# Attention scores computed once in a two-layer transformer kernel

## The chip, the cores and the metric

The kernel runs on one core of one Trainium2 chip. The metric is the device time of one launch in microseconds. Before the change it is 2117.11 us, the median of two runs (2116.69 and 2117.53).

## The reference

The input x has 2048 tokens of 640 features. Two layers follow, with the same weights, and each layer has two residual blocks:

```python
x = x + _A_ref(_layernorm(x, axis=-1), A_wqkv, A_wo)   # attention
x = x + _B_ref(_layernorm(x, axis=-1), B_w1, B_b1, B_w2, B_b2)   # token mixer
```

Attention has 32 heads of 20 features. For each head it computes scores = q @ k^T / sqrt(20) over 2048 x 2048 pairs, their softmax, the product with v, and at the end a projection with `wo`. The mixer normalizes again, multiplies over the token axis with `w1` (2048 x 1536), adds a bias, applies a gelu, and multiplies back with `w2`.

## The kernel before

**Layout.** Heads are padded from 20 to 32 rows, so that four heads of a group fill 128 partitions; there are 8 groups. K (`KT`) and Q (`QTq`) are kept transposed, features on partitions. A score matmul works on 64 rows, which hold two heads. Masked copies of Q (`qev`, `qod`, made by `prep_block`) zero one of the two, so that one 64-row matmul gives the scores of a single head. Heads 0 and 1 use rows 0 to 63, heads 2 and 3 rows 64 to 127, and the order 0, 2, 1, 3 makes neighbours use different halves of the array, where they run side by side.

**Units, chunks and tiles.** A unit is one block of 512 queries, one group and one block of 128 keys: 4 x 8 x 16 = 512 units in a layer. Each unit gives four chunks, one for each head, of 128 keys x 512 queries. Three chunks in a row make a tile `S` of three PSUM banks, so that a layer has 683 tiles, four tiles for three units. There are two `S` buffers, six banks; the accumulator `acc` and the tile `misc` have one bank each.

**The loop of attention.** In the step for tile t, `attention` emits, in this order: the score matmuls of tile t+1 (`emit_S`, L317); the exponential of tile t on ScalarE (`emit_exp`, L345), which writes `P`; the product with V (`emit_PV`, L551) for every unit whose last tile is at least one step old, four matmuls that use 32 columns of the array each and run side by side; and then some fill matmuls (`emit_fills`). TensorE's order is fixed: every matmul is chained to the one before it. The scores of tile t+1 must wait until the exponential of tile t-1 has left their buffer, and an exponential waits for the last score matmul of its tile.

**Fills.** Work of TensorE that is not part of the loop above is queued and fed in between: projections of K and Q for later groups and blocks (L223), the output projection (L453, L486) and three quarters of the mixer's first multiplication (L426). A step without a P.V group takes up to 3 cost units of it, and one with a P.V group up to 1.5; a unit is a matmul of 512 columns. When a group of fill matmuls ends, VectorE copies it from `misc` and one step is left without fills. Where the queue is empty, or its first item not due, there are none either: in the profile the longest such stretches run from 456 to 515 us and from 678 to 746 us, and at 1505 and 1727 us in the second layer.

**The second pass.** Before a tile's scores are emitted, `planned_fill` says whether the current step will have fills. If not, `emit_S` runs with `reps` of 1: it issues the tile's three score matmuls twice, the second time over the same PSUM banks with the same result.

```python
has_fill = planned_fill()
reps = 0 if has_fill else CFG["R_DEFAULT"]
if t + 1 < NTILES:
    emit_S(t + 1, reps)
```

**Start.** GpSimd sets up the identity matrix for the transposes, two small constants, two bias transfers (L118, L119) and the rstd of each LayerNorm (L165) in one queue.

Of the kernel before, what the change touches and what calls it, by code (L numbers as in the profile page):

```python
# [11 lines left out]
BF16 = mybir.dt.bfloat16  # L12
# [12 lines left out]
VW = 24  # L25

CFG = dict(
    R_DEFAULT=1,
    FILL_NOPV=3.0,
    FILL_PV=1.5,  # L30
    PV_LAGT=1,
# [8 lines left out]
def kernel(  # L40
# [12 lines left out]
    nc = tc.nc  # L53
# [11 lines left out]
    def pe(inst):  # L65
        tc.chain_iter_dep("pe_order", inst.ins)
        return inst
# [12 lines left out]
    consts = ctx.enter_context(tc.tile_pool(name="consts", bufs=1))  # L80
# [16 lines left out]
    warm = consts.tile([128, 1], F32, name="warm")  # L97
    nc.gpsimd.tensor_tensor(out=warm[:], in0=mhalf[:], in1=mhalf[:], op=ALU.mult)
    nc.gpsimd.tensor_tensor(out=warm[:], in0=warm[:], in1=mhalf[:], op=ALU.pow)
    x1lp = ctx.enter_context(tc.tile_pool(name="x1lp", bufs=1))  # L100
    x1last = x1lp.tile([128, 4, D], F32, name="x1last")
    hhp = ctx.enter_context(tc.tile_pool(name="hhp", bufs=1))
# [137 lines left out]
    def attention(st, x_in_ap, x_mid, uacc_l):  # L240
        layer = st.layer
        KT, hT = st.KT, st.hT
        with ExitStack() as p1:
# [19 lines left out]
            S_tiles, P_tiles, acc_tiles, qm_tiles, attnT_tiles = {}, {}, {}, {}, {}  # L263
# [21 lines left out]
            def on_unit_start(n):  # L285
                qb_n, g_n, kt_n = units[n]
                fill_state["unit"] = n
                if qb_n == 0 and kt_n == 0:
                    if g_n + KQA < NG:
                        enqueue_kq_for_group(g_n + KQA)  # L290
                    if g_n == max(0, NG - KQA) and NQB > 1:
                        enqueue_qproj(1)
                if qb_n >= 1 and g_n == 0 and kt_n == 2 and qb_n + 1 < NQB:
                    enqueue_qproj(qb_n + 1)
                if not proj_enqueue_done[0]:
                    last_k_block = max(0, NG - 1 - KQA)
                    if NQB == 1:
                        done = (qb_n == 0 and g_n >= last_k_block)
                    elif NQB == 2:
                        done = (qb_n == 0 and g_n >= max(0, NG - KQA)) or qb_n >= 1  # L300
                    else:
                        done = (qb_n == NQB - 2 and (g_n > 0 or kt_n >= 2)) or qb_n > NQB - 2
                    proj_enqueue_done[0] = done
                check_hT_dead()
                if kt_n == 0:
                    ensure_ready(qb_n, g_n)
                    prep_block(qb_n, g_n)
                if kt_n == NKT // 2 and n + NKT < NU:
                    nqb, ng, _ = units[n + NKT - kt_n]
                    if ("Q", nqb, ng) not in pending_keys():  # L310
                        prep_block(nqb, ng)

            def s_matmul(St, slot, n, j):
                qb, g, kt = units[n]
                jj = j // 2
                q = qm_tiles[(qb, g)][j % 2]
                pe(nc.tensor.matmul(St[:, slot, :], lhsT=KT[64 * jj:64 * jj + 64, g, kt * 128:(kt + 1) * 128],  # L317
                                    rhs=q[64 * jj:64 * jj + 64, :], start=True, stop=True,
                                    tile_position=(64 * jj, 0)))

            def emit_S(t, reps):
                cs = chunks[3 * t:3 * t + 3]
                for (n, j) in cs:
                    if j == HORDER[0]:
                        on_unit_start(n)
                St = sps.tile([128, 3, 512], F32, name="S")
                S_tiles[t] = St
                for _rep in range(reps + 1):
                    i = 0
                    while i < len(cs):  # L330
                        n, j = cs[i]
                        if i + 1 < len(cs) and cs[i + 1][0] == n and (j, cs[i + 1][1]) in ((0, 2), (1, 3)):
                            s_matmul(St, i, n, j)
                            s_matmul(St, i + 1, n, cs[i + 1][1])
                            i += 2
                        else:
                            s_matmul(St, i, n, j)
                            i += 1

            def emit_exp(t):  # L340
                St = S_tiles.pop(t)
                ncs = len(chunks[3 * t:3 * t + 3])
                P = ptp.tile([128, 3, 512], BF16, name="P")
                P_tiles[t] = P
                nc.scalar.activation(out=P[:, 0:ncs, :].rearrange("p a b -> p (a b)"),  # L345
                                     in_=St[:, 0:ncs, :].rearrange("p a b -> p (a b)"),
                                     func=ACT.Exp, scale=SCALE)
# [194 lines left out]
            def emit_PV(n):  # L542
                qb, g, kt = units[n]
                if kt == 0:
                    acc_tiles[(qb, g)] = accp.tile([128, 512], F32, name="acc")
                acc = acc_tiles[(qb, g)]
                for j in range(4):
                    ci = 4 * n + HORDER.index(j)
                    P = P_tiles[ci // 3]
                    hh = 4 * g + j  # L550
                    pe(nc.tensor.matmul(acc[32 * j:32 * j + 32, :],  # L551
                                        lhsT=Vaug[:, (kt * H + hh) * VW:(kt * H + hh) * VW + 32],
                                        rhs=P[:, ci % 3, :], start=(kt == 0), stop=(kt == NKT - 1),
                                        tile_position=(0, 32 * j)))
                for t_ in list(P_tiles.keys()):
                    if (3 * t_ + 2) // 4 <= n:
                        del P_tiles[t_]
                if kt == NKT - 1:
                    normalize(qb, g, acc_tiles.pop((qb, g)))
                    if qb == LASTQB and PARTIAL_LAST:  # L560
                        if g % 2 == 1:
                            enqueue_outproj_partial(qb, g)
                    elif g == NG - 1:
                        enqueue_outproj(qb)

            def emit_fills(budget, pool_alloc):
                fs = fill_state
                if fs["cooldown"] > 0:
                    fs["cooldown"] -= 1
                    return 0.0  # L570
                spent = 0.0
                while spent < budget:
                    if fs["cur"] is None:
                        if not fill_queue:
                            break
                        if fill_queue[0].get("not_before", 0) > fs["unit"] and budget < 100:
                            break
                        fs["cur"] = fill_queue.popleft()
                        fs["idx"] = 0
                        fs["tile"] = pool_alloc()  # L580
                    grp = fs["cur"]
                    grp["mms"][fs["idx"]](fs["tile"])
                    spent += grp["cost"][fs["idx"]]
                    fs["idx"] += 1
                    if fs["idx"] == len(grp["mms"]):
                        grp["evac"](fs["tile"])
                        fs["cur"] = None
                        fs["cooldown"] = CFG["FILL_GAP"]
                        break
                return spent  # L590
# [4 lines left out]
            def planned_fill():  # L595
                if fill_state["cooldown"] != 0:
                    return False
                if fill_state["cur"] is not None:
                    return True
                return len(fill_queue) > 0 and fill_queue[0].get("not_before", 0) <= fill_state["unit"]  # L600

            LAGT = CFG["PV_LAGT"]
            pv_done = 0
            emit_S(0, 0)
            for t in range(NTILES):
                has_fill = planned_fill()
                reps = 0 if has_fill else CFG["R_DEFAULT"]
                if t + 1 < NTILES:
                    emit_S(t + 1, reps)
                emit_exp(t)  # L610
                n_pv = 0
                while pv_done < NU and (4 * pv_done + 3) // 3 <= t - LAGT:
                    emit_PV(pv_done)
                    pv_done += 1
                    n_pv += 1
                emit_fills(CFG["FILL_PV"] if n_pv else CFG["FILL_NOPV"], misc_alloc)
            in_attention[0] = False
            while pv_done < NU:
                emit_PV(pv_done)
# [148 lines left out]
    with ExitStack() as a_stack:  # L768
        st0 = open_a_scope(0, a_stack)
        with ExitStack() as p0:  # L770
# [29 lines left out]
            setup_wo()  # L800
            setup_biases()
        attention(st0, A_x[0], xd[0], uacc[0])
    with ExitStack() as a_stack:
        st1 = open_a_scope(1, a_stack)
# [59 lines left out]
```

## Time and profile before

| | |
|---|---|
| median of two runs | 2117.11 us |
| span of the profiled execution, first to last instruction | 2114.4 us |
| its distance to the two timed runs | 2.3 and 3.1 us |
| TensorE busy | 1950.4 us (92%), 13278 matmuls |
| ScalarE busy | 1934.5 us (91%), 1508 instructions |
| VectorE busy | 623.7 us (29%) |
| GpSimd busy | 166.4 us (8%) |
| mean granted TensorE clock | 0.990 |
| chain that ended last: the exponential (L345) | 56% of the span |
| the same: score matmuls (L317) | 11% |

The profiled execution has no time of its own beside the span; the table sets the span against the timed runs. Attention takes 48 to 972 us in the first layer and 1097 to 2021 us in the second; the start, the mixers and the end fill the rest. In the rows of tenths each digit is a fortieth of the span, about 53 us. The clock row shows which share of TensorE's full clock was granted. In the lines of groups, the numbers after the bar are the busy time of the group, the mean length of one in ns, and the idle time before them with what ended most of it. Instructions of one engine overlap, so the busy time is less than count times length: 1366 exponentials of 1501 ns are busy for 1839.6 us. The length of a matmul includes its flight through the array, so that a matmul of 512 columns is listed with about 0.38 us while the next can start after 0.215 us.

### The profile page before, as it was taken

The page shows a single profiled execution, that of the slowest core. Times are in us where ns is not written, and L with a number is a line of the kernel's source. Part 1 is how long each engine was busy: PE and PEld are TensorE (multiplying, and loading weights), DVE is VectorE, ACT ScalarE, POOL GpSimd, SP SyncE. Part 2 cuts the span into 40 slices and gives each one's busy share as a digit, 9 for nine tenths or more (in the row PEclk, how much of TensorE's full clock was granted, in tenths as well). Part 3 has the DMA queues.
Part 4 walks back from the last instruction along what each step waited for, and adds up shares of the span by engine and source line. Part 5 has one row for each costly group of instructions (what it writes and reads, how often), then busy time and mean ns, then how long its engine had stood idle before and what let it go on. Part 6 is the DMA issues. An engine that isn't in the chain of part 4 may idle for free.

```text
span 2114.4 us, 32063 instructions
## 1 busy us (share of the span) xinstructions
PE 1950.4 (92%) x13278; PEld 655.8 (31%) x13278; DVE 623.7 (29%) x1391; ACT 1934.5 (91%) x1508; POOL 166.4 (8%) x250
## 2 busy tenths in 40 slices
PE   7999999999999999996999999999999999999969
PEld 4222222233223323222542222222332233232235
DVE  6122233212422042223642122432123221422252
ACT  5999999999999999995349999999999999999952
POOL 2000000110012001100000000001000110111000
PEclk9999999999999999998999999999999999999989
DMA  5000000110034012223620000101100430232145
GB/s 129 1 1 1 1 20 19 63 51 10 29 64 64 1 38 43 39 40 96 212 81 1 1 1 1 38 21 65 41 26 26 75 53 1 57 53 37 32 120 181
DMA packets 90739, 96.89 MB, mean 46 GB/s; under 512 B 9696, under 2 KB 68192, under 8 KB 90592
## 3 DMA queue, kind: packets, MB, share of 16 engines
q1 hardware_dynamic: 70464, 71.22, 10.9%
q0 software_dynamic: 20128, 23.62, 7.4%
q8 instruction: 104, 1.70, 0.3%
q14 instruction: 43, 0.35, 0.1%
HBM read 55.48 MB, written 39.32 MB: 45 GB/s over the span
## 4 chain that ended last, share of the span: by engine, by line
ACT 56%; PE 26%; issue 12%; DVE 3%; DMA 1%; POOL 0%; SPq 0%; POOLq 0%; ACTq 0%; DVEq 0%
ACT P L345 56%; PE S L317 11%; PE y L746 4%; PE acc L551 4%; PE misc L223 3%; PE pp L214 1%; PE misc L453 1%; DVE bnst L158 1%; DMA ua<-uacc_65 0%; DVE bnst L159 0%; DMA ua<-uacc_66 0%; POOL rstd L165 0%; PE S L486 0%; DVE utmp L685 0%; PE pp L223 0%
## 5 line engine op out<-in xcount | busy, mean ns | idle before, releaser
L345 ACT ACTIVATE P<-S 128x1536 bf16<-128x1536 f32 (+1 forms) x1366 | 1839.6, 1501 | 9.8 <-PE S L317 8.3
L317 PE MATMUL S<-qev,KT 64*128 64x512 bf16 x2962 | 836.2, 377 | 97.4 <-ACT P L345 91.6
L317 PE MATMUL S<-qod,KT 64*128 64x512 bf16 x3052 | 838.0, 379 | 7.9 <-ACT P L345 3.7
L317 PEld LDWEIGHTS <-KT 64*128 64x128 bf16 x6014 | 326.4, 93 | 657.0 <-issue 487.8
L551 PE MATMUL acc<-P,Vaug 128*32 128x512 bf16 x4096 | 409.9, 389 | 6.2 <-ACT P L345 1.9
L551 PEld LDWEIGHTS <-Vaug 128*32 128x32 bf16 x4096 | 106.5, 92 | 439.0 <-issue 439.0
L432 DVE COPY ustg<-misc 128x512 f32<-128x512 f32 (+1 forms) x144 | 70.0, 486 | 291.8 <-PE misc L426 291.7
L165 POOL TENSOR_TENSOR rstd<-veps,mhalf 128x1 f32<-128x1 f32 x96 | 54.0, 563 | 1194.1 <-DVE veps L163 1167.1
L426 PE MATMUL misc<-h2st,w1st 128*128 128x512 bf16 (+1 forms) x576 | 116.1, 303 | 1.8 <-DVE h2st L170 1.8
L746 PE MATMUL y<-uT,w2s 128*128 128x512 bf16 (+1 forms) x768 | 107.6, 299 | 3.4 <-ACT uT L689 1.4
L513 DVE CAST QTq<-misc 128x512 bf16<-128x512 f32 x62 | 42.8, 691 | 205.5 <-PE misc L223 205.5
L513 DVE CAST KT<-misc 128x512 bf16<-128x512 f32 x56 | 38.7, 691 | 212.0 <-PE misc L223 207.8
L223 PE MATMUL misc<-hh,wq_pad 128*128 128x512 bf16 x310 | 98.9, 385 | 0.0
L276 DVE TENSOR_SCALAR qev<-QTq,mask_ev 128x512 bf16<-128x512 bf16 x64 | 22.5, 352 | 228.7 <-PE S L317 228.2
L223 PE MATMUL misc<-hh,wk_pad 128*128 128x512 bf16 x280 | 87.2, 385 | 0.0
L453 PE MATMUL misc<-wo_pad,attnT 128*128 128x512 bf16 (+1 forms) x384 | 76.8, 303 | 0.0
L746 PEld LDWEIGHTS <-w2s 128*128 128x128 bf16 x768 | 59.6, 98 | 49.9 <-issue 5.1
L76 ACT CAST Vaug<-pp 128x500 bf16<-128x500 f32 (+1 forms) x32 | 14.3, 453 | 50.8 <-PE pp L214 50.8
L437 POOL DMA_DIRECT2D uacc_66<-ustg x48 | 41.3, 860 | 232.7 <-DVE ustg L432 215.3
L437 POOL DMA_DIRECT2D uacc_65<-ustg x48 | 41.3, 861 | 232.4 <-DVE ustg L432 219.9
L426 PEld LDWEIGHTS <-w1st 128*128 128x128 bf16 x576 | 33.9, 97 | 61.1 <-issue 58.8
L462 DVE TENSOR_TENSOR x1s<-misc,xin 128x512 f32<-128x512 f32 (+1 forms) x48 | 23.5, 489 | 98.1 <-PE misc L453 98.1
(455 smaller groups left out, 839.6 us busy)
## 6 DMA issues: line engine op xcount, KB each, us to landing
w2s<-in_B_w_dram SPq DMA_DIRECT2D x16, 768.0 KB
w1st<-in_B_w_dram SPq DMA_DIRECT2D x36, 256.0 KB
uacc_65<-ustg POOLq DMA_DIRECT2D x36, 256.0 KB, 3.9
uacc_66<-ustg POOLq DMA_DIRECT2D x36, 256.0 KB, 4.0
xd_63<-x1s SPq DMA_DIRECT2D x24, 320.0 KB
x1in<-xd_63 SPq DMA_DIRECT2D x24, 320.0 KB
xd_64<-x2s SPq DMA_DIRECT2D x16, 320.0 KB
xin<-xd_64 SPq DMA_DIRECT2D x16, 320.0 KB
```

The costliest lines, as they stand in the source:

```text
L165: nc.gpsimd.tensor_tensor(out=rstd[:], in0=veps[:], in1=mhalf[:], op=ALU.pow)
L223: pe(nc.tensor.matmul(t[:, :], lhsT=wpad[:, dt_, g, :], rhs=st.hT[:, dt_, tb * 512:(tb + 1) * 512], start=(dt_ == 0), stop=(dt_ == NDT - 1)))
L317: pe(nc.tensor.matmul(St[:, slot, :], lhsT=KT[64 * jj:64 * jj + 64, g, kt * 128:(kt + 1) * 128], rhs=q[64 * jj:64 * jj + 64, :], start=Tru ...
L345: nc.scalar.activation(out=P[:, 0:ncs, :].rearrange("p a b -> p (a b)"), in_=St[:, 0:ncs, :].rearrange("p a b -> p (a b)"), func=ACT.Exp, ...
L426: pe(nc.tensor.matmul(t[:, 0:w], lhsT=states[fp]["w"][:, sti, ftl * 128:(ftl + 1) * 128], rhs=tiles4[sti][:, c0:c1], start=(sti == 0), sto ...
L432: nc.vector.tensor_copy(out=stg[:, 0:w], in_=t[:, 0:w])
L437: nc.gpsimd.dma_start(out=dst, in_=stg[:, 0:w], accum_op=ALU.add)
L453: pe(nc.tensor.matmul(t[:, 0:w], lhsT=attnT[:, g, ttl * 128:(ttl + 1) * 128], rhs=wo_pad[:, g, c0:c1], start=(g == 0), stop=(g == NG - 1)))
L462: nc.vector.tensor_tensor(out=x1s[:, c0:c1], in0=t[:, 0:w], in1=ts_["xin"][:, c0:c1], op=ALU.add)
L513: nc.vector.tensor_copy(out=dst_ap, in_=t[:, :])
L551: pe(nc.tensor.matmul(acc[32 * j:32 * j + 32, :], lhsT=Vaug[:, (kt * H + hh) * VW:(kt * H + hh) * VW + 32], rhs=P[:, ci % 3, :], start=(kt ...
L746: pe(nc.tensor.matmul(y[:, 0:w], lhsT=w2s[:, ft, sl * 128:(sl + 1) * 128], rhs=uT[:, ft, c0:c1], start=(ft == 0), stop=(ft == NF - 1)))
```

## The change

Every score tile is computed once: the argument `reps` and the loop over it are gone. The order of the score matmuls within a tile is the same as before. A new function `keep_busy` can add matmuls of zero weights to the open accumulators in steps without fills; its count, `N_KEEP`, is 0, so it emits none. Its two operands are allocated and set by GpSimd at the start. In the built program TensorE has 1918 matmuls and 1918 weight loads fewer, and its order is otherwise unchanged; on GpSimd there are two memsets more, and the two bias transfers stand later, after the third rstd.

```diff
 CFG = dict(
-    R_DEFAULT=1,
+    N_KEEP=0,
...
+    zw = consts.tile([128, 128], BF16, name="zw")
+    nc.gpsimd.memset(zw[:], 0.0)
+    zr = consts.tile([128, 512], BF16, name="zr")
+    nc.gpsimd.memset(zr[:], 1.0)
...
-            def emit_S(t, reps):
+            def emit_S(t):
...
-                for _rep in range(reps + 1):
-                    i = 0
-                    while i < len(cs):
-                        n, j = cs[i]
-                        if i + 1 < len(cs) and cs[i + 1][0] == n and (j, cs[i + 1][1]) in ((0, 2), (1, 3)):
-                            s_matmul(St, i, n, j)
-                            s_matmul(St, i + 1, n, cs[i + 1][1])
-                            i += 2
-                        else:
-                            s_matmul(St, i, n, j)
-                            i += 1
+                for i, (n, j) in enumerate(cs):
+                    s_matmul(St, i, n, j)
+
+            def keep_busy(count):
+                for acc in acc_tiles.values():
+                    for _ in range(count):
+                        pe(nc.tensor.matmul(acc[:], lhsT=zw[:], rhs=zr[:], start=False, stop=False,
+                                            skip_group_check=True))
...
-            emit_S(0, 0)
+            emit_S(0)
             for t in range(NTILES):
                 has_fill = planned_fill()
-                reps = 0 if has_fill else CFG["R_DEFAULT"]
                 if t + 1 < NTILES:
-                    emit_S(t + 1, reps)
+                    emit_S(t + 1)
...
                 emit_fills(CFG["FILL_PV"] if n_pv else CFG["FILL_NOPV"], misc_alloc)
+                if not has_fill:
+                    keep_busy(CFG["N_KEEP"])
```

## The prediction

> **What bounds the kernel now.** I read the page's engine totals, the chain that ended last and the costliest groups first, then the trace's timeline and its sums by stretch.
>
> ```profile
> PE   7999999999999999996999999999999999999969
> ACT  5999999999999999995349999999999999999952
> PEclk9999999999999999998999999999999999999989
> L345 ACT ACTIVATE P<-S 128x1536 bf16<-128x1536 f32 (+1 forms) x1366 | 1839.6, 1501 | 9.8 <-PE S L317 8.3
> L317 PE MATMUL S<-qev,KT 64*128 64x512 bf16 x2962 | 836.2, 377 | 97.4 <-ACT P L345 91.6
> L317 PE MATMUL S<-qod,KT 64*128 64x512 bf16 x3052 | 838.0, 379 | 7.9 <-ACT P L345 3.7
> ```
>
> In both attention passes ScalarE is never free: the exponential (L345) keeps it busy for 1839.6 of 2114.4 us and waits 9.8 us in all. TensorE is as full in the tenths, but that is not need: it waits for ScalarE (91.6 us), and 2962 + 3052 = 6014 score matmuls ran where 2 layers x 512 units x 4 heads = 4096 give all scores. The other 1918 are the second pass. The clock row is 9 wherever attention runs.
>
> A stretch without fill work, in TensorE's timeline (start, length, line, tile, count):
>
> ```profile
> 467.76 0.37 PE L317 MATMUL S<-qev,KT 64*128 64x512 bf16 x1 [0.32 <-ACT P L345]
> 467.76 0.60 PE L317 MATMUL S<-qod,KT 64*128 64x512 bf16 x3
> 468.19 0.38 PE L317 MATMUL S<-qev,KT 64*128 64x512 bf16 x1
> 468.40 0.38 PE L317 MATMUL S<-qod,KT 64*128 64x512 bf16 x1
> 468.71 0.40 PE L551 MATMUL acc<-P,Vaug 128*32 128x512 bf16 x4
> 469.10 0.39 PE L317 MATMUL S<-qev,KT 64*128 64x512 bf16 x2
> ```
>
> Six score matmuls (three and their repeats) take 0.95 us until the P.V group follows; that group of four runs side by side and hands on after 0.39 us. A stretch with fills, where the score tile is computed once:
>
> ```profile
> 1108.31 0.39 PE L317 MATMUL S<-qod,KT 64*128 64x512 bf16 x1
> 1108.31 0.60 PE L317 MATMUL S<-qev,KT 64*128 64x512 bf16 x2
> 1108.84 0.40 PE L551 MATMUL acc<-P,Vaug 128*32 128x512 bf16 x4
> 1109.17 0.60 PE L223 MATMUL misc<-hh,wk_pad 128*128 128x512 bf16 x2
> 1109.71 0.39 PE L317 MATMUL S<-qod,KT 64*128 64x512 bf16 x2
> ```
>
> Three score matmuls hand on after 0.53 us, P.V after 0.33, two fills after 0.54. Both stretches repeat every four tiles, in 5.37 us (1.34 us per exponential).
>
> **Part 1, the removal at full clock.** The 1918 matmuls and as many weight loads go; TensorE's order is otherwise unchanged. The exponential waits for a tile's last score matmul, so in repeated tiles it is ready 0.43 us sooner. That is hidden by the exponential before it, except where TensorE was late. From the starts of all exponentials: ahead of a repeated tile they are 1.370 us apart on average (638 of them), ahead of a single one 1.338 (724). The gain lies between 0 and 638 x 0.032 = 20 us; I take 12, by the 9.8 us that ScalarE waits and a part of the rest.
>
> **Part 2, the clock, which decides.** What the second pass also did was to keep TensorE occupied. The same trace has the slow clock elsewhere. Ten matmuls of 3200 columns together, before the clock first rises and after:
>
> ```profile
> 12.60 2.85 PE L214 MATMUL pp<-wv,hh 128*128 128x500 bf16 x10 [0.84 <-DVE hh L78]
> 17.70 1.52 PE L214 MATMUL pp<-wv,hh 128*128 128x500 bf16 x10
> ```
>
> Less the time of flight (0.20 and 0.16 us), 512 columns hold the array for 0.42 us slow and 0.215 us fast. Twice the clock fell and came back 20.5 us later. I read such places in stretches of 3.4 us, a sixth of that (columns: TensorE busy and matmuls, granted clock, DMA):
>
> ```profile
> 1087.89:1091.30 3.41, 1.78 (x18) 1.00 0.24 96
> 2019.97:2023.38 3.41, 1.36 (x9) 1.00 0.61 177
> 2026.80:2030.21 3.41, 2.27 (x9) 0.50 0.89 222
> 2040.46:2043.87 3.41, 3.36 (x13) 0.50 0.09 14
> ```
>
> After the first the clock stayed; after the second it fell; after the third it did not rise; after the fourth it did. Counted as array time (columns x 0.215/512, half for a score matmul on 64 rows, a quarter for a P.V matmul on 32 columns), the four are 44%, about 23% (records of a few are missing), 57% of slow array time, and 98%. So the clock falls at some share between 23 and 44%, and returns at one between 57 and 98%.
>
> Without the second pass, four tiles without fills hold 12/2 + 3 = 9 array times, 9 x 0.215 = 1.94 of 5.37 us: 36%, inside the gap (before: 15 x 0.215 = 3.2, 60%). Single stretches of 3.4 us go from 28 to 46%. Counted by busy time, 1.36 of 3.41 (40%) fell and 1.78 (52%) held, and the new pattern would keep 4 x 0.60 + 3 x 0.40 = 3.6 less overlaps, over 60%: above the row that held. The two measures disagree; I lean a little to array time.
>
> [...] The trace speaks against gap length as the measure: by the timeline, the clock fell in the second stretch after idle times of 0.41, 0.53 and 1.1 us. [...]
>
> **Part 3, price if the clock falls.** Hand-overs cost 0.09 us (scores to P.V), 0.175 (P.V to scores), 0.12 (to fills, and from them 0.11). No row shows them at the slow clock; between once and twice these, I take 1.2 times, by the time of flight (0.20 to 0.16).
> - *No fills*: four score runs of two array steps, 4 x (0.85 + 0.11), and three P.V, 3 x (0.425 + 0.21): 5.75 us per four tiles against 5.37, +0.10 per tile (ends 0.05 and 0.27). The long stretches without fill matmuls (456 to 515, 678 to 746, 941 to 972, and their like at 1505, 1727 and 1991) hold 314 / 1.343 = 233 tiles: **+23** (12 to 63).
> - *Fills return, clock still low*: four score runs, three P.V, five fills in three groups, about 3.85 + 1.9 + 5 x 0.425 + 0.4 = 8.3 us against 5.37. A spell of 3.4 us loses 35%, 1.2 us. One or two spells at each of four returns: **+7** (5 to 10).
> - *Dips among the fills*: with the limit midway between 28 and 44%, 11 stretches outside the long ones lie below it, 11 x 1.2 = **+13** (0, to 82 for the 68 below 44%).
> - Part 1: **-12** (0 to -20).
>
> Sum +31, on the profiled 2114.4 us and the 2.7 us around it (median 2117.11): **2148**, case range 2114 to 2272.
>
> **The rest.** The loop of the new function runs zero times, and its two operands are only set: two memsets on GpSimd (the 128x128 one of its kind took 0.20 us), which then waits until 6.95 us for its first rstd. Both bias issues (1.22 and 1.36 us) now stand behind the third rstd, ahead of the fourth: 0 to 1 us late at the start; I take 0, since VectorE is full there. No wait is added; VectorE, ScalarE and SyncE keep their order.
>
> **Rivals.**
> - *The clock holds*: Part 1 alone, 2097 to 2117, about 2105. For it: the busy-time measure, and 36% being nearer to 44 than to 23. Against: single stretches at 28%.
> - *The clock falls and does not come back* (the slower side). With fills, slow TensorE is full, yet its array share is only (6 + 3 + 5) x 0.425 / 8.3 = 72%, inside 57 to 98%. If the return asks for more, TensorE becomes the bound and tiles with fills take 8.3/4 = 2.07 us in place of 1.34. From the first long stretch to the last fills in each pass, 2 x 426 us x 0.54 = 460, plus 23: about 2600. All of attention slow: 1133 x 2.07 + 233 x 1.44 = 2680 for 1846, 2950; a few lost spells, 2270. It decides from the point where a fill stretch at the low clock no longer lifts it.
>
> **How the numbers follow.** Clock falls and returns 0.36 (forecast 2148); holds 0.34; stays low 0.28; another cause 0.02. About 2%, 42 us, is what can be told from no change: above 2159 lie the third case and 0.16 of the first, 0.44 in all; faster than 2075 only 0.02; within, 0.54. The range 2092 to 2500 leaves out some 0.16 of the third case above and little below; the likeliest's own is 2114 to 2272.
>
> **What would show it.** The clock row: below 9 in the slices around 456 to 515, 678 to 746, 1505 and 1727 us and back within a few us of the fills (forecast); 9 throughout and exponentials 1.33 to 1.34 us apart (holds); 5 into the fill stretches with ScalarE waiting for L317 or fills (stays low). Score matmul counts must fall to 4096; single runs of three must hand on after about 0.96 us where the clock is low. I am wrong if the clock weighs something that neither measure shows, or if slow hand-overs are far from 1.2 times.

## The result and the profile after

The changed kernel takes 2134.43 us (2131.76 and 2137.10) against 2117.11 us: 1.0078 times the time before, 95% interval 1.0059 to 1.0097. It is slower, by less than the 2% that the prediction took as its bound. The profiled execution has a span of 2135.3 us, 20.9 more than before, and a mean granted clock of 0.913 in place of 0.990.

The changed kernel's page, in tenths and groups, as shown of before:

```profile
PE   7888888889888987776998888888898889877769
ACT  5999999999999999995449999999999999999952
PEclk9989999986999599996999999999769985999969
L346 ACT ACTIVATE P<-S 128x1536 bf16<-128x1536 f32 (+1 forms) x1366 | 1846.1, 1693 | 24.6 <-PE S L321 19.0
L321 PE MATMUL S<-qev,KT 64*128 64x512 bf16 x2048 | 649.0, 415 | 200.6 <-ACT P L346 191.9
L321 PE MATMUL S<-qod,KT 64*128 64x512 bf16 x2048 | 647.8, 417 | 73.9 <-ACT P L346 69.3
```

The score matmuls are down to 4096, and TensorE waits for ScalarE more than twice as long as before (261.2 us against 95.2 in its waits). Yet the mean length of a score matmul went up, from 378 to 416 ns: part of them ran at half clock (granted clock 0.50 from 488 to 522 us). The clock row drops to 5 or 6 in the slices around 500, 720, 1570 and 1790 us, the long stretches without fills; where attention ends it is 6 in place of 8. ScalarE now waits 19.0 us for scores, against 8.3.

In the long stretches the timeline of TensorE (start, length, line, tile, count) reads:

```profile
486.23 0.62 PE L552 MATMUL acc<-P,Vaug 128*32 128x512 bf16 x4
486.78 0.61 PE L321 MATMUL S<-qod,KT 64*128 64x512 bf16 x2
487.19 1.30 PE L321 MATMUL S<-qev,KT 64*128 64x512 bf16 x2
487.91 1.00 PE L321 MATMUL S<-qod,KT 64*128 64x512 bf16 x2
488.84 0.62 PE L552 MATMUL acc<-P,Vaug 128*32 128x512 bf16 x4
489.41 0.61 PE L321 MATMUL S<-qev,KT 64*128 64x512 bf16 x2
489.80 0.63 PE L321 MATMUL S<-qod,KT 64*128 64x512 bf16 x1
490.35 0.62 PE L552 MATMUL acc<-P,Vaug 128*32 128x512 bf16 x4
490.90 0.60 PE L321 MATMUL S<-qod,KT 64*128 64x512 bf16 x1
```

P.V hands on after about 0.55 us, three score matmuls after 0.96 us and the scores of two tiles in a row after 2.06 us (486.78 to 488.84), without a wait: TensorE has become the bound there. Four tiles take 2.06 + 0.55 + 0.96 + 0.55 + 0.96 + 0.55 = 5.63 us against 5.37. Where the low clock meets fills it is worse. TensorE's lines first, then one of ScalarE:

```profile
135.72 1.03 PE L321 MATMUL S<-qev,KT 64*128 64x512 bf16 x2
136.67 0.62 PE L552 MATMUL acc<-P,Vaug 128*32 128x512 bf16 x4
137.22 1.03 PE L227 MATMUL misc<-hh,wk_pad 128*128 128x512 bf16 x2
138.19 0.61 PE L321 MATMUL S<-qod,KT 64*128 64x512 bf16 x2
```

```profile
136.84 1.45 ACT L346 ACTIVATE P<-S 128x1536 bf16<-128x1536 f32 x1 [0.95 <-PE S L321]
```

From one score run to the next 2.48 us pass, and ScalarE is idle for 0.95 of them.

The whole difference lies in the two attention passes, which take 935.5 and 933.8 us against 923.8 and 924.1 (+21.4); the rest together is 0.5 us shorter. The distances between the starts of neighbouring exponentials, sorted by the clock in force midway between them, give the account against the 1.353 us that they average before. The long stretches are here the six that lie between two fill matmuls at least 30 us apart or between the last fill and the end of attention:

| exponentials in attention | count | mean distance, us | against before, us |
|---|---|---|---|
| full clock | 1142 | 1.341 | -14.0 |
| low clock, inside the six long stretches | 189 | 1.417 | +12.1 |
| low clock, at the ends of these, in the same spells | 8 | 2.27 | +7.4 |
| low clock, spells elsewhere among the fills | 25 | 2.00 | +16.0 |
| sum | 1364 | | +21.5 |

So the second pass had cost some 12 ns per tile, and its removal gains that back. The low clock takes more, 35.5 us, and two thirds of its price fall on the 33 exponentials outside the long stretches.

### The profile page after: what moved, and what is told of

Its sections match the earlier page's. It is cut to its first block, busy times and chain, and to the rows that moved or that the text cites. A ratio compares the mean times of both kernels' runs of the same rounds, so it can differ in the third digit from the quotient of the medians.

```text
span 2135.3 us, 28229 instructions
## 1 busy us (share of the span) xinstructions
PE 1809.2 (85%) x11360; PEld 537.8 (25%) x11360; DVE 624.1 (29%) x1391; ACT 1941.4 (91%) x1508; POOL 167.7 (8%) x252
## 4 chain that ended last, share of the span: by engine, by line
ACT 68%; PE 16%; issue 12%; DVE 3%; DMA 1%; POOL 1%; SPq 0%; ACTq 0%; POOLq 0%; DVEq 0%
ACT P L346 67%; PE y L748 4%; PE S L321 4%; PE acc L552 2%; PE misc L227 1%; PE pp L218 1%; PE misc L454 1%; PE big L677 1%; POOL rstd L169 1%; DVE bnst L162 1%; DVE bnst L163 0%; PE S L487 0%; PE pp L227 0%; DVE x1last L500 0%; DVE utmp L687 0%
## 5 line engine op out<-in xcount | busy, mean ns | idle before, releaser
L321 PE MATMUL S<-qev,KT 64*128 64x512 bf16 x2048 | 649.0, 415 | 200.6 <-ACT P L346 191.9
L321 PE MATMUL S<-qod,KT 64*128 64x512 bf16 x2048 | 647.8, 417 | 73.9 <-ACT P L346 69.3
L552 PE MATMUL acc<-P,Vaug 128*32 128x512 bf16 x4096 | 445.9, 424 | 0.6 <-ACT P L346 0.6
L321 PEld LDWEIGHTS <-KT 64*128 64x128 bf16 x4096 | 207.6, 95 | 729.9 <-issue 705.2
L438 POOL DMA_DIRECT2D uacc<-ustg x96 | 83.2, 867 | 463.9 <-DVE ustg L433 426.2
L355 DVE STREAM_TRANSPOSE T<-acc 128x512 f32<-128x512 f32 x64 | 45.8, 716 | 188.8 <-PE acc L552 188.8
L218 PE MATMUL pp<-wv,hh 128*128 128x500 bf16 (+1 forms) x320 | 50.4, 307 | 1.6 <-DVE hh L78 1.6
```

The source lines that it names most:

```text
L218: pe(nc.tensor.matmul(pp[:, 0:c1 - c0], lhsT=st.hT[:, dt_, tt * 128:(tt + 1) * 128], rhs=wv[:, dt_, c0:c1], start=(dt_ == 0), stop=(dt_ == ...
L438: nc.gpsimd.dma_start(out=dst, in_=stg[:, 0:w], accum_op=ALU.add)
L552: pe(nc.tensor.matmul(acc[32 * j:32 * j + 32, :], lhsT=Vaug[:, (kt * H + hh) * VW:(kt * H + hh) * VW + 32], rhs=P[:, ci % 3, :], start=(kt ...
```

## The experiments

**Theory:** the loss is the low clock, and the clock goes by how full TensorE is in each stretch of about 3.4 us; at full clock the change is a gain. **Rivals:** the start or the single score runs are what costs; the isolated dips, not the long stretches, carry the loss; the clock goes by some other measure of being busy.

**e1, a zero matmul of 512 elements in the steps without fills.**

```diff
-    N_KEEP=0,
+    N_KEEP=1,
```

> The changed kernel with one matmul of zero weights (128 rows, 128 columns, 512 elements) in each step without fills, 600 in all. Theory (the low clock is what costs, and the lost second pass gains 14 to 17 us): array share without fills goes from 36 to over 50%, the clock row is 9 throughout attention, exponentials stay at 1.33 to 1.34 us, 2097 to 2106 us. Rival (the loss comes from single score runs or from the start, not from the clock): no better than the changed kernel, 2130 us or more, even at full clock.

Measured: 2108.4 us (2103.7 to 2116.4), 0.9965 times before (0.9951 to 0.9979). Its page:

```profile
PEclk9999999999999999998999999999999999999989
L346 ACT ACTIVATE P<-S 128x1536 bf16<-128x1536 f32 (+1 forms) x1366 | 1834.7, 1783 | 2.6 <-PE S L321 2.6
```

The clock row is that of the kernel before, ScalarE's wait for scores falls to 2.6 us, and the loss has turned into a gain of 8 us with score tiles computed once. The low clock (mean 0.989 here, 0.913 in the changed kernel) was the cause. The time is 2 us over the expected range: exponentials average 1.344 us, not 1.341, and three of the ten executions had a lower mean clock (0.981 to 0.983), so there was probably a low spell in each; they have no trace. The added matmul is not in every such step: `keep_busy` writes to open accumulators, and once an accumulator has been finished there is none until the next is opened, one or two steps later (600 matmuls for some 640 steps). What these holes do is shown with e9 below.

**e4, the kernel before with the second pass switched off and nothing else.**

```diff
-    R_DEFAULT=1,
+    R_DEFAULT=0,
```

> The kernel before with the second pass switched off and nothing else: no memsets on GpSimd, bias transfers where they were. Theory: the start is worth 0 to 1 us, so this is the changed kernel's time, 2130 to 2138 us, with its low spells. Rival (the start costs several us): 2125 us or less.

Measured: 2139.2 us (2132.3 to 2141.9), ratio 1.0097 (1.0076 to 1.0118), clock 0.910. The median is 1 us above the expected range, and the executions overlap with the changed kernel's two. Without the memsets nothing is gained: the start is no part of the loss.

**e5 and e6, the second pass in half of its places.** e5 keeps it where no fill is due, e6 in the one step after each fill group.

```diff
-                reps = 0 if has_fill else CFG["R_DEFAULT"]
+                reps = 0 if (has_fill or fill_state["cooldown"] != 0) else CFG["R_DEFAULT"]   # e5
+                reps = CFG["R_DEFAULT"] if fill_state["cooldown"] != 0 else 0                 # e6
```

> The kernel before with the second pass only where the fill queue has nothing due (281 tiles), not in the one step that follows each fill group. Theory: no low spells in the long stretches; the isolated dips among the fills stay, 15 us in the changed kernel's trace; against the kernel before the repeats gone among the fills gain about 11 us: 2112 to 2124 us.

> The other half: the second pass only in the step after each fill group (358 tiles). Theory: no dips among the fills, low clock through the six long stretches, which cost 233 tiles x 0.07 us and some 2 us at each of four returns, 24 us: 2130 to 2142 us. Rival (the dips are what costs, the long stretches are hidden behind ScalarE): 2117 us or less.

Measured: e5 2109.4 us, ratio 0.9962 (0.9949 to 0.9975), 3 us below the expected range; e6 2135.5 us, ratio 1.0090 (1.0074 to 1.0107). The clock rows, e5 first:

```profile
PEclk9999999999999999998999999999999999999889
```

```profile
PEclk9999999986999599995999999999779985999869
```

With the second pass in the long stretches alone the clock holds nearly everywhere (mean 0.985); with it after the fill groups alone the long spells are back (0.918) and so is the loss. The long stretches, with the entry of the low clock into the fills at their ends, are enough for the loss, and the rival by which the dips alone are what costs falls. The dips are not free: in the changed kernel's profile they stand for 16.0 us (table above). e5 does nothing against them, but its profile has only four isolated low stretches of 3.4 us among the fills and one spell of 13.7 us that runs into the last long stretch, which fits its better time; why they were fewer is not shown. In this kernel the second pass after fill groups was a cost.

**e7, the zero matmul only where no fill is due.**

```diff
-                if not has_fill:
+                if not has_fill and not gap_step:
                     keep_busy(CFG["N_KEEP"])
```

Here `gap_step` is true in the step after a fill group.

> The changed kernel with the zero matmul of 512 elements only where the fill queue has nothing due. Theory: the long stretches hold the clock, the dips among the fills remain: 2103 to 2120 us, between e1 and e5.

Measured: 2111.8 us, ratio 0.9986 (0.9958 to 1.0013), inside the expected range but not between e1 and e5, and from 2102.1 to 2131.5: the mean clock of an execution lay between 0.970 and 0.992, and the slowest one, which is the one profiled, had a spell of 44 us in the first long stretch. Once the clock is low, the added matmul makes it dearer: exponentials were 1.92 us apart in that spell, against 1.42 in the long stretches of the changed kernel.

**e2, e9, e3 and e8, what the clock counts.** The same step as e1 with another zero matmul:

```diff
-  matmul(acc[:], lhsT=zw[:], rhs=zr[:], ...)                                         # e1: 128 rows, 128 columns, 512 elements
+  matmul(acc[:, 0:128], lhsT=zw[:], rhs=zr[:, 0:128], ...)                           # e2: 128 elements
+  matmul(acc[:, 0:256], lhsT=zw[:], rhs=zr[:, 0:256], ...)                           # e9: 256 elements
+  matmul(acc[0:32, :], lhsT=zw[:, 0:32], rhs=zr[:], tile_position=(0, 0), ...)       # e3: 32 columns
+  matmul(acc[:], lhsT=zw[0:32, :], rhs=zr[0:32, :], tile_position=(0, 0), ...)       # e8: 32 rows
```

> The same with 128 elements in place of 512: a quarter of the array time. Theory: the share without fills goes from 36 to about 40%, the edge of what held in the changed kernel's trace, so low spells remain but are fewer: 2103 to 2125 us, clock 0.93 to 0.98. If the mere presence of a matmul in every step counted, it would be as e1.

> The same with 512 elements but 32 of the array's 128 columns: as long on TensorE as e1, as much of the array as e2. If the clock goes by array share (columns and rows counted), it behaves as e2: low spells, 2103 to 2125 us. If it goes by the time in which any matmul streams, it behaves as e1: no low spells, 2097 to 2106 us.

> As e1, 512 elements, but with weights of 32 rows and all 128 columns. If the clock goes by rows in use (score matmuls of 64 rows counting half, P.V counting fully), the share without fills rises from 36 to 40% only, inside the range where stretches fell in the earlier traces: long low spells, in which each added matmul costs 0.42 us and a hand-over of TensorE's time: 2180 to 2290 us. If any streaming counts, as e1 and e3: no low spells, 2100 to 2110 us.

> As e1 with 256 elements in place of 512, all rows and columns: share without fills 44%. No stretch over 42% has fallen in the earlier traces: few or no low spells, 2100 to 2112 us. If the limit lies higher or an added matmul disturbs by itself, as e2 with 128 elements: 2130 us or more.

| | us | ratio to before (95%) | clock, profiled |
|---|---|---|---|
| e1, 128 rows x 128 columns, 512 | 2108.4 | 0.9965 (0.9951 to 0.9979) | 0.989 |
| e3, 128 rows x 32 columns, 512 | 2105.9 | 0.9951 (0.9937 to 0.9966) | 0.990 |
| e8, 32 rows x 128 columns, 512 | 2227.6 | 1.0531 (1.0500 to 1.0562) | 0.899 |
| e9, 128 x 128, 256 | 2131.7 | 1.0085 (1.0068 to 1.0101) | 0.980 |
| e2, 128 x 128, 128 | 2158.5 | 1.0198 (1.0171 to 1.0225) | 0.912 |

e3 and e8 stand on TensorE for the same 512 elements and use the same quarter of the array; one holds the clock (its profile has one low stretch of 3.4 us in attention), the other loses it. The pages, e3 first:

```profile
PEclk9999999999999999998999999999999999999989
L346 ACT ACTIVATE P<-S 128x1536 bf16<-128x1536 f32 (+1 forms) x1366 | 1834.9, 1755 | 3.7 <-PE S L321 3.5
L338 PE MATMUL acc<-zr,zw 128*32 128x512 bf16 x600 | 228.8, 381 | 0.0
```

```profile
PEclk9999999975998589995999999999579985999869
L346 ACT ACTIVATE P<-S 128x1536 bf16<-128x1536 f32 (+1 forms) x1366 | 1855.8, 1678 | 100.1 <-PE S L321 96.9
L338 PE MATMUL acc<-zr,zw 32*128 32x512 bf16 x600 | 270.6, 451 | 0.0
```

So the share that fits these runs counts a matmul's time by the rows in use and not by its columns: a score matmul of 64 rows counts half, one of 32 columns fully. Array share fell as the measure with e3, time of any matmul with e8. Rows in use and values streamed into the array per unit of time are the same number in all these runs, so which of the two counts stays open.

Why e8 and e2 are far slower than the changed kernel, which adds nothing: in the low spells TensorE is the bound (at a granted clock of 0.50 it is busy for 20.00 of 20 us, in e8 from 495 to 515 and in e2 from 490 to 510 us), and the added matmul is paid in full. e8's timeline there:

```profile
501.30 0.60 PE L338 MATMUL acc<-zr,zw 32*128 32x512 bf16 x1
501.84 0.61 PE L321 MATMUL S<-qev,KT 64*128 64x512 bf16 x2
502.24 0.63 PE L321 MATMUL S<-qod,KT 64*128 64x512 bf16 x1
502.80 0.62 PE L552 MATMUL acc<-P,Vaug 128*32 128x512 bf16 x4
503.35 0.60 PE L338 MATMUL acc<-zr,zw 32*128 32x512 bf16 x1
```

The addition takes 0.54 us, and a tile 2.05. Its exponentials at low clock are 1.92 us apart on average, e2's 1.64, the changed kernel's 1.51.

All low spells in these traces last whole multiples of 3.41 us (twice 20.48 us before the change, 3.41 to 68.27 us in the changed kernel), but for those that the end of the kernel cuts off. So each profile can be cut into stretches of 3.41 us, laid on the clock's switching times, and each stretch gets a share by rows: a matmul of 512 columns counts 0.215 us at full and 0.43 us at low clock (back-to-back ones of 128 rows start 0.216 us apart at full and 0.38 to 0.43 at low clock, before and after), times its rows out of 128, and matmuls side by side in different columns count once. Nine profiles have a record of every matmul (before, after, e1 to e4, e8 to e10); those of e5 to e7 lack 160 to 187 and are left out. The share sorts the outcomes so:

| share by rows, at full clock | fell | held |
|---|---|---|
| under 0.36 | 61 | 1 |
| 0.36 to 0.38 | 21 | 9 |
| 0.38 to 0.39 | 2 | 32 |
| 0.39 and over | 0 | 4835 |

At the low clock, none of 530 stretches under 0.73 was followed by the full clock, 22 of 50 between 0.73 and 0.75, and all 53 above. About 0.37 for the fall and 0.74 for the return are estimates from these counts. The other two measures sort worse: 30 held stretches lie below the highest row share that fell, 80 by array share, 792 by the time of any matmul.

e2 and e9 were misses. I had reckoned with the mean share (40 and 44%), but the clock falls on a single stretch: e9's profiled execution fell twice inside attention, after stretches of 0.38 and 0.33, and stayed low for 37.5 us the first time; its other executions had clocks of 0.955 to 0.962. Both falls lie where an accumulator has just been finished and the added matmul is missing in two steps. Some of TensorE's lines ahead of the first, which came at 483.82 us:

```profile
478.91 0.28 PE L338 MATMUL acc<-zr,zw 128*128 128x256 bf16 x1
479.92 0.40 PE L552 MATMUL acc<-P,Vaug 128*32 128x512 bf16 x4
480.74 0.39 PE L321 MATMUL S<-qod,KT 64*128 64x512 bf16 x2 [0.43 <-ACT P L346]
482.09 0.37 PE L321 MATMUL S<-qev,KT 64*128 64x512 bf16 x1 [0.76 <-ACT P L346]
482.61 0.40 PE L552 MATMUL acc<-P,Vaug 128*32 128x512 bf16 x4
482.94 0.28 PE L338 MATMUL acc<-zr,zw 128*128 128x256 bf16 x1
```

From 478.91 to 482.94 us, 4.0 us, no matmul is added. The 44 us spell of e7 and the one low stretch of e3 begin at the same kind of place. No run closes these holes. What e2 costs while low was left out of its expectation.

**e10, provoking a clock that stays low.** One small matmul in each step *with* fills, none elsewhere:

```diff
-                if not has_fill:
+                if has_fill:
                     keep_busy(CFG["N_KEEP"])     # 32 rows, 128 columns, 128 elements
```

> The rival that the clock stays low, provoked: the changed kernel with one small matmul (32 rows, 128 columns, 128 elements) in each step with fills, 680 in all, none elsewhere. At full clock it is hidden: 4 x (0.054 + 0.11) us on top of some 4.5 of 5.37 us per four tiles. At the low clock TensorE is full with fills, and the addition lowers its share from 72 to about 66%. If the clock returns only at some 75%, it now stays low through much of the fills: 2250 to 2750 us, exponentials 2.1 to 2.4 us apart there. If being busy without a break brings it back: within 20 us of the changed kernel, 2130 to 2155 us.

Measured: 2132.1 us (2129.8 and 2134.4), ratio 1.0071 (1.0051 to 1.0091), no different from the changed kernel. Its clock row:

```profile
PEclk9999999985999599995999999999769995999969
```

The clock came back with the fills as before. Its last low stretches ahead of a return inside attention had row shares of 0.73 to 0.78, not the 0.66 that I had worked out for the steady mix. The provocation missed its mark, so the state that stays low all through the fills was not seen; it is not shown impossible.

**The fastest versions.** Three kernels of this study beat both the kernel before and the changed one: e3 (0.9951 of before), e5 (0.9962) and e1 (0.9965). Their intervals overlap.

## Why the prediction was right

**The way and the case.** The forecast was that the clock falls in the stretches without fills and comes back with the fills: 2148 us, with 2114 to 2272 for this case. It was 2134.4. The clock row shows the falls in the places that were named, and e1 and e4 show that they are the cause. The choice of the case was partly luck. It had a chance of 0.36, hardly more than the two rivals, and it rested on a lean to array time, which is not what the clock goes by: e3 shows that columns do not count (clock 0.990 with 32 of them, 0.989 in e1 with 128). In the kernels before and after, array time and rows in use give nearly the same share, since score matmuls use all 128 columns and four P.V matmuls usually run side by side, so the wrong measure gave the right answer. The prediction had named this as a way of being wrong, that the clock weighs something that neither of its measures shows.

**Part 1** (12 us of gain, 0 to 20): measured 14.0 us on 1142 exponentials at full clock.

**The limits of the fall.** The stretch read as about 23% has no missing records (13278 matmuls and as many weight loads are there): its P.V groups come in parts of two and three. It is 14 to 16% by array time and 22% by rows. The limit found, about 37%, lies in the predicted gap of 23 to 44% all the same.

**Long stretches** (+23): +12.1. This term was sized too large twice over. The cycle of four tiles took 5.63 us, not 5.75: a single score run hands on after 0.96 us, exactly as priced, and two in a row take 2.06 us in place of 1.92, but P.V hands on after 0.55 us, not 0.635. The hand-over from P.V to the scores is thus not dearer than the 0.12 us to a fill, and the 0.175 read before held a wait for ScalarE: in the lines of the prediction the score runs start 1.34 us apart (467.76 and 469.10), as the exponentials do. And 189 tiles were low, not 233, since the clock falls some way into a stretch.

**Returns** (+7): +7.4 at the ends of the long stretches. A four-tile cycle with fills was priced at 8.3 us, 2.07 per tile; single tiles with two fills take 2.48, others less, and these eight 2.27 in the mean.

**Dips among the fills** (+13): +16.0. Eleven stretches had been counted as below the limit. Seven spells came, two of them of four stretches (13.7 us), together 13 stretches.

**The sum** of +31 stands against +20.9 of the profiled execution and +17 of the medians; the difference is mainly the term of the long stretches.

**The rivals.** "The clock holds" fell, and with it the busy-time measure that spoke for it: in the changed kernel stretches with TensorE busy for 63% of the time fell. Its price for attention at full clock was nearly right: e3 ran at 2105.9 us, where 2105 had been worked out. "The clock does not come back" did not happen, as the fills lift the share to about 0.74 or above within one to four stretches. That margin is small, since single stretches without fills at low clock reach 0.74 too and stay low.

**Gap length.** The prediction read the trace of before as speaking against gap length as the measure, and the changed kernel agrees: TensorE's longest wait for ScalarE in it is 0.8 us, as the waits show (waiting line, releaser, total, times, longest),

```profile
PE S L321 <- ACT P L346: 261.2, 628, 0.8
```

and the clock fell in attention all the same.

**The start** (0 to 1 us): the first exponential starts at 48.5 us, 0.15 later than before.

## What to carry to other kernels

Work that looks redundant on an engine that is not the bound may be what keeps its clock up, as here (0.990 with the second pass, 0.913 without): before it is taken out, compute the share of time that is left, stretch by stretch, with a matmul counted by its rows, as fitted these runs (e3 and e8), and compare the lowest stretch, not the mean, with places in the same trace where the clock fell or held. Where a filler was needed here, one with full rows and few columns in the steps that lack work did it (e3: 0.990, 2105.9 us), and it replaced real work done twice (2117.11 us); the fillers that did not hold the clock were worse than none, because they were paid in full once it had fallen (e2 2158.5 us, e8 2227.6, against 2134.4). In these runs it was needed in every step that lacks work: 4.0 us without it, two steps, came before the first fall of e9, and the spell of e7 begins at such a place. When the granted clock drops to half, as here to 0.50, sum the engine's own cycle, hand-overs included (5.63 us against 5.37 here), to see whether it becomes the bound.

## What the runs showed of the hardware

- The granted clock went by rows in use, not by columns: with the same elements and the same quarter of the array, 128 rows x 32 columns held it (0.990, 2105.9 us) and 32 rows x 128 columns did not (0.899, 2227.6 us).
- Zero weights served: the added matmuls of e1 multiply by zero and still held the clock (0.989, 2108.4 us).
- The fall and the return lay far apart in these traces, near shares of 0.37 and 0.74 (estimates from the counts above). As a matmul of 512 columns counts 0.43 us at the low clock in place of 0.215, the 0.36 of the steps without fills became 0.61 to 0.74 in the long stretches of the changed kernel and did not bring the clock back: it stayed low, for 68 us in the longest spell, until 1.2 to 5.9 us after the next fills began in the four stretches that fills follow.
